# A narrow product as four column strips of TensorE, and a plan with its own durations for ACT and DVE, in a fused attention and MLP kernel

## The chip, the cores and the metric

One core of a Trainium2 chip. The metric is the device time of one execution in microseconds. The engines are named as the profile names them: PE (TensorE), PEld (its weight loads), DVE (VectorE), ACT (ScalarE), POOL (GpSimd), SP (SyncE). PSUM is the memory that takes the matmuls' results in this kernel; a ring is a fixed number of buffers that are used in turn. The granted clock is the share of PE's full clock that the profile records. The verdict "faster" begins at 2%.

## The reference

```python
# q, k, v: (8, 12, 448, 64) float32; U: (448, 32); V: (32, 448)
q_n = q / (norm(q) + 1e-6);  k_n = k / (norm(k) + 1e-6)
attn = softmax(q_n @ k_n.T / tau)
x = (attn @ v) with the heads side by side             # (8, 448, 768)
h = x.transpose(0, 2, 1) @ U @ V                       # low rank, over the sequence
u = x + h.transpose(0, 2, 1)
out = u + relu(u @ w_ch1) @ w_ch2                      # 768 -> 3072 -> 768
```

## The kernel before

The kernel does not issue instructions where it describes them. It adds operations to a plan; a list scheduler in Python gives each a start by estimated durations, and the instructions are issued in that order. The engines work through their own lists in order, so a number in the plan moves instructions on all of them. The plan counts buffers too: a matmul that takes a buffer of a ring waits in the plan until one is free. Cuts are marked with `# ...`.

```python
def pe_t(n):  return n / 2400.0 + 0.0025
def act_t(n, fixed=0.10):  return fixed + n * 0.00083
def dve_t(n, fast=1, fixed=0.16):  return fixed + n * 0.00104 / fast
# ...
r_mm = ring(3, [128, 512], FP, "mm", psum)      # three PSUM buffers: U, V, transposes, both MLP layers
r_sc = ring(3, [128, 512], FP, "sc", psum)      # three for the scores
U_sb = const.tile([128, 2, 4, 128], BF, name="U_sb")   # U's 32 columns, padded by zeros to 128
# ... in stage0(b), by column parts (512, 128, 128 in batches 0 and 1, 384, 384 later):
for t in range(4):                               # A = U^T x, summed over four parts of the sequence
    plan.add(Op("PE", pe_t(c1 - c0), lambda ...: nc.tensor.matmul(
        out=mm.tile[:, 0:c1 - c0], lhsT=U_sb[:, par, t, :], rhs=X.tile[:, t, c0:c1],
        start=(t == 0), stop=(t == 3)), ...))
a = Op("ACT/DVE", act_t(c1 - c0), None, ...)     # copy A out of PSUM; then V^T A, and u = x + it on DVE
# ... in mlp(b):
side = 3 if b == 0 else 1                        # output tiles of the second layer done together
# ... the constants:
nc.scalar.copy(out=U_sb[:, par, :, 0:R], in_=U_f()[:, par])
nc.scalar.copy(out=V_sb[0:R, PAD:PAD + S].rearrange("r (c s) -> r s c", c=SC),
               in_=V_f().rearrange("r (s c) -> r s c", c=SC))
```

Of the kernel before, what the change touches and what calls it, by code (L numbers as in the profile page):

```python
# [20 lines left out]
PAD = 64  # L21
# [28 lines left out]
class Plan:  # L50
# [5 lines left out]
    SEM = 0.10  # L56
    SAFE = 0.25

    def __init__(self):
# [40 lines left out]
    def run(self):  # L100
# [22 lines left out]
        while left:  # L123
# [6 lines left out]
            while progress:  # L130
                progress = False
                for e in self.ENGINES:
# [34 lines left out]
                    o.start, o.by = t, e  # L167
                    o.end = t + o.dur
                    free[e] = o.end
                    if isinstance(o.lat, tuple):  # L170
                        q, work, fixed = o.lat
                        dma[q] = max(dma[q], o.end) + work
                        o.end = dma[q] + fixed
                    else:
                        o.end += o.lat
# [23 lines left out]
def kernel(  # L199
# [79 lines left out]
    def U_f():  # L279
        return uv.tile[:, 0:8 * R].rearrange("p (b t r) -> p b t r", b=2, t=4)  # L280

    def V_f():
        return uv.tile[0:R, 8 * R:]

# [6 lines left out]

    U_sb = const.tile([128, 2, 4, 128], BF, name="U_sb")
    V_sb = const.tile([128, PAD + S + PAD], BF, name="V_sb")
# [25 lines left out]
    def pe_t(n):  # L319
        return n / 2400.0 + 0.0025  # L320

    def act_t(n, fixed=0.10):
        return fixed + n * 0.00083

    def dve_t(n, fast=1, fixed=0.16):
        return fixed + n * 0.00104 / fast

# [22 lines left out]
    def flip(stream, ins, n, into, part, deps, acq, rel):  # L350

        tp = Slot(r_mm, 1)
        tp.own = True
        for z, x in enumerate(ins):
            def fn(z=z, x=x):
                if z == 0:
                    tp.tile = psum.tile([128, len(ins), n], BF, name="tp", tag="mm", bufs=3)
                nc.tensor.transpose(out=tp.tile[:, z, :], in_=x(), identity=ident[:n, :n])  # L358
            o = plan.add(Op("PE", 0.06, fn, deps=deps + [id_set] if z == 0 else (), acq=[tp] + acq,
                            rel=rel if z == len(ins) - 1 else []), stream)  # L360
        c = plan.add(Op("ACT/DVE", dve_t(n * len(ins), 2), None, deps=[o], acq=acq, rel=[tp],
                        prio=0.2, fast=True))
        c.fn = lambda: copy_op(c, *part(into(), tp.tile))
        return c
# [36 lines left out]
    def load_v0(h0, h1):  # L401

        o = load(lambda: nc.gpsimd.dma_start(
            out=v_raw()[:, h0:h1, :], in_=v[0, h0:h1].rearrange("h (s c) d -> s h (c d)", c=SC)),
            (h1 - h0) * 0.5, acq=[raw])
        c = plan.add(Op("ACT/DVE", dve_t(256 * (h1 - h0), 2), None, deps=[o, v0_set], prio=0.35,
                        fast=True))
        c.fn = lambda: copy_op(c, v_first()[:, h0:h1, :, 0:D],
                               v_raw()[:, h0:h1, :].rearrange("p h (c d) -> p h c d", c=SC))
        for h in range(h0, h1):  # L410
            got[0, h, "v"] = [c]

    def stats(b, h0, h1, ld, ops):
# [5 lines left out]
        for i in range(2):  # L419
            for a0 in range(0, g, G // 2):  # L420
                a1 = min(g, a0 + G // 2)
                sq = Slot(r_sq, 1)
                o = Op("ACT/DVE" if b == 0 else "DVE", dve_t(256 * (a1 - a0), 2, 0.10), None,
                       deps=[ops[i]], acq=[sq], prio=pr + 0.2, fast=True)

                def square(o=o, i=i, a0=a0, a1=a1, sq=sq):
# [12 lines left out]
                    deps=[o], acq=[ss], rel=[sq], prio=pr + 0.1)))  # L439
        o = plan.add(Op("ACT", act_t(32), lambda: nc.scalar.activation(  # L440
            ln.tile[:, :, 0:g, :], ss.tile[:, :, 0:g, :], AF.Ln),
            deps=red, acq=[ln], rel=[ss], prio=0))
        o = plan.add(Op("ACT", act_t(32), lambda: nc.scalar.activation(
            nv.tile[:, :, 0:g, :], ln.tile[:, :, 0:g, :], AF.Exp, scale=0.5),
            deps=[o], acq=[nv], rel=[ln], prio=0))
        o = plan.add(Op("DVE", dve_t(32), lambda: nc.vector.tensor_scalar_add(
            nv.tile[:, :, 0:g, :], nv.tile[:, :, 0:g, :], EPS), deps=[o], prio=pr))
        o = plan.add(Op("DVE", dve_t(32), lambda: nc.vector.reciprocal(
            inv.tile[:, :, 0:g, :], nv.tile[:, :, 0:g, :]), deps=[o], acq=[inv], rel=[nv], prio=pr))
# [5 lines left out]
    def norm(b, p, ld, inv, a, deps, pr):  # L455
# [7 lines left out]
        def part(i, hh):  # L463
            def fn():
# [5 lines left out]
                else:  # L470
                    dst = xn.tile[:, 4 * hh:4 * hh + 4, 64 * hh:64 * hh + 64]
                    nc.vector.tensor_mul(dst, src[:, hh], sc[:, hh].to_broadcast([SCH, SC, D]))  # L472
            return plan.add(Op("DVE", dve_t(512 if i == 0 else 256, fixed=0.08), fn, deps=deps, acq=[xn],
                               rel=[ld, inv] if (i, hh) != (1, 0) else [ld, inv], prio=pr))
# [16 lines left out]
    def attention(b, p, X):  # L491
# [19 lines left out]
        for hh in range(2):  # L511
# [3 lines left out]
            for t in range(4):  # L515
                for j in range(4):
                    first, last = t == 0 and j == 0, t == 3 and j == 3
                    def fn(t=t, j=j, h=h, hh=hh, av=av):
# [8 lines left out]
                        rel=([attn, raw] if small and hh else [attn]) if last else []), pe_av)  # L527
            r = plan.add(Op("DVE", dve_t(4), lambda av=av, rd=rd: nc.vector.reciprocal(  # L528
                out=rd.tile, in_=av.tile[:, :, D:D + 1]), deps=[o], acq=[rd], prio=1))
# [4 lines left out]
        last_av[b, p] = o  # L534
        return muls


    prev = {}

    def stage0(b, X, muls):  # L540
# [5 lines left out]
        for c0, c1 in cols:  # L546
            mm = Slot(r_mm, 1)
            need = [m for i, m in enumerate(muls) if i * D < c1]
            for t in range(4):
                o = plan.add(Op("PE", pe_t(c1 - c0), lambda t=t, c0=c0, c1=c1, mm=mm: nc.tensor.matmul(  # L550
                    out=mm.tile[:, 0:c1 - c0], lhsT=U_sb[:, par, t, :], rhs=X.tile[:, t, c0:c1],
                    start=(t == 0), stop=(t == 3)),
                    deps=need + consts[:2 + par] if t == 0 else (), acq=[mm, A] if t == 0 else []),
                    pe_a if c1 < C else pe_av)
            a = Op("ACT/DVE", act_t(c1 - c0), None, deps=[o], rel=[mm], prio=0)
            a.fn = lambda a=a, c0=c0, c1=c1, mm=mm: copy_op(
# [64 lines left out]
    def mlp(b, us, uT, ut):  # L621
# [5 lines left out]
        for f in range(NC):  # L627
            mm = Slot(r_mm, 1)
            for cc in range(CC):
# [4 lines left out]
                    acq=[mm] if cc == 0 else [], rel=[uT]), pe_mlp)  # L634
            r = Op("ACT/DVE", act_t(n, 0.17), None, deps=[o], acq=[relu], rel=[mm],
                   prio=0)
# [64 lines left out]
    def zero():  # L701
        nc.vector.memset(U_sb, 0.0)
        nc.vector.memset(V_sb, 0.0)

    zf = fill(lambda: nc.vector.memset(U_f(), 0.0), 256, prio=-4, acq=[uv])
    z = fill(zero, 1500, prio=-0.2)

# [12 lines left out]
    def cast_u(par):  # L720
        nc.scalar.copy(out=U_sb[:, par, :, 0:R], in_=U_f()[:, par])

    def cast_v():
        nc.scalar.copy(out=V_sb[0:R, PAD:PAD + S].rearrange("r (c s) -> r s c", c=SC),
                              in_=V_f().rearrange("r (s c) -> r s c", c=SC))

# [17 lines left out]
    u0 = load_u(0)  # L744
    v0 = plan.add(Op("SP", 0.45, lambda: nc.sync.dma_start(out=V_f(), in_=moe_V), acq=[uv], prio=-2, lat=2.5))
    u1 = load_u(1)
# [8 lines left out]
    for i in range(NW):  # L755
        w1_ops.append(load_w1(i, NW))
    consts = [plan.add(Op("ACT", 0.25, lambda: cast_u(0), deps=u0 + [z], rel=[uv], prio=3)),
              plan.add(Op("ACT", 0.5, cast_v, deps=[v0, z], rel=[uv], prio=3)),
              plan.add(Op("ACT", 0.25, lambda: cast_u(1), deps=u1 + [z], rel=[uv], prio=3))]
# [55 lines left out]
```

## Time and profile before

| | before |
|---|---|
| median time | 628.89 us (628.43 to 629.86, 3 runs) |
| span of the profiled run | 625.9 us |
| PE, DVE, ACT busy | 95%, 50%, 46% |
| first matmul, first score matmul, first MLP matmul | 11.15, 13.58, 50.30 us |

The last row is read from PE's timeline. The chain's piece of MLP matmuls starts at 50.46. The batches go in pairs for the MLP; "the V stage" is the stretch in which batch 1's U, V and transposes run, near 92 to 104 us.

The windows of the kernel before, columns: window, length, busy us and count of PE, PEld, DVE, ACT and POOL, granted clock of PE, DMA share, GB/s.

```profile
85.00:95.00 10.00, 9.85 (x123) 6.45 (x121) 5.45 (x15) 7.91 (x18) 9.05 (x15) 1.00 1.40 113
95.00:105.00 10.00, 7.46 (x53) 4.48 (x52) 8.93 (x23) 2.78 (x5) 0.00 (x0) 0.83 0.10 7
105.00:115.00 10.00, 10.00 (x63) 6.00 (x62) 9.69 (x24) 0.92 (x4) 1.41 (x2) 1.00 0.59 83
```

In the second window PE is idle for a quarter of the time and its granted clock is 0.83 (0.50 from 99 to 101 us), while DVE is busy for nine tenths.

### The profile page before, as it was taken

How to read it: one execution, taken by the hardware profiler on the slowest of the kernel's cores; microseconds unless marked ns; L12 is line 12 of the kernel's file. 1: busy time of each engine (PE TensorE's matmuls, PEld its weight loads, DVE VectorE, ACT ScalarE, POOL GpSimd, SP SyncE). 2: the span in 40 equal slices, each digit the busy share in tenths (PEclk: the TensorE clock that was granted, in tenths of full speed). 3: DMA queues.
4: the chain of work that ended last, by engine and by line, in shares of the span. 5: the costliest groups of instructions: out<-in, count | busy, mean ns of one | idle time of the engine just before them, and what ended most of it. 6: DMA issues, size and time to landing. Idle time of an engine off the chain costs nothing.

```text
span 625.9 us, 11519 instructions
## 1 busy us (share of the span) xinstructions
PE 595.8 (95%) x4704; PEld 354.4 (57%) x4704; DVE 310.5 (50%) x763; ACT 286.2 (46%) x604; POOL 109.6 (18%) x168
## 2 busy tenths in 40 slices
PE   1799998999999999999999999999999999999997
PEld 1465665565555566666544666666544666654464
DVE  7876969999999888754650244014400220010011
ACT  6984782277874058424843048513543005104300
POOL 6227160152343303400320000000000000000000
PEclk9999998999999999999999999999999999999999
DMA  9999991999798968942781224030002310310011
GB/s 124 192 205 130 210 149 10 159 145 183 88 146 121 164 131 112 138 76 58 120 81 24 66 49 92 1 76 27 27 1 32 57 51 1 76 51 1 0 51 51
DMA packets 145733, 54.41 MB, mean 87 GB/s; under 512 B 109488, under 2 KB 145680, under 8 KB 145680
## 3 DMA queue, kind: packets, MB, share of 16 engines
q0 software_dynamic: 69216, 25.96, 37.2%
q1 hardware_dynamic: 76464, 27.71, 23.2%
q8 instruction: 37, 0.61, 0.4%
q14 instruction: 16, 0.13, 0.1%
HBM read 52.08 MB, written 11.01 MB: 101 GB/s over the span
## 4 chain that ended last, share of the span: by engine, by line
PE 81%; DVE 12%; ACT 3%; DMA 2%; SPq 1%; issue 1%; DVEq 0%; ACTq 0%
PE mm L630 32%; PE mm L653 30%; PE sc L503 9%; PE av L521 7%; DVE ss L435 2%; DVE xn L472 2%; PE mm L550 2%; DVE xn L469 1%; DVE sq L431 1%; PE mm L578 1%; ACT attn L507 1%; SPq L715 1%; DMA raw_uv<-in_moe_U_dram 1%; DMA out_dram<-O_sb 1%; DVE u_nat L592 1%; DVE X_sb L530 1%
## 5 line engine op out<-in xcount | busy, mean ns | idle before, releaser
L630 PE MATMUL mm<-uT,w_sb 128*128 128x512 bf16 (+1 forms) x1152 | 238.6, 353 | 1.2 <-DVE qkT L683 0.5
L653 PE MATMUL mm<-w_sb,relu 128*128 128x384 bf16 x1344 | 233.2, 326 | 1.5 <-DVE O_sb L663 0.7
L507 ACT ACTIVATE attn<-sc 128x448 bf16<-128x448 f32 (+1 forms) x342 | 160.8, 552 | 90.9 <-PE av L521 61.6
L653 PEld LDWEIGHTS <-relu 128*128 128x128 bf16 x1344 | 131.3, 98 | 92.6 <-issue 4.3
L630 PEld LDWEIGHTS <-w_sb 128*128 128x128 bf16 x1152 | 112.6, 98 | 104.5 <-issue 3.4
L640 ACT ACTIVATE relu<-mm 128x512 bf16<-128x512 f32 (+1 forms) x173 | 94.2, 545 | 158.6 <-PE mm L630 158.4
L663 DVE TENSOR_TENSOR O_sb<-mm,u_nat 128x384 f32<-128x384 f32 x56 | 30.8, 555 | 236.1 <-PE mm L653 231.7
L503 PE MATMUL sc<-qkT 128*128 128x448 bf16 (+1 forms) x342 | 102.3, 360 | 5.6 <-ACT attn L507 3.7
L521 PEld LDWEIGHTS <-attn 128*128 128x128 bf16 (+1 forms) x1536 | 61.0, 98 | 17.1 <-issue 2.9
L435 DVE TENSOR_REDUCE ss<-sq 112x8 f32<-112x512 bf16 x96 | 65.4, 683 | 4.3 <-ACT sq L429 1.7
L394 POOL DMA_DIRECT2D v_nat<-in_v_dram x98 | 63.1, 651 | 22.5 <-DMA w_sb<-in_moe_w_ch_dram 5.9
L521 PE MATMUL av<-v_nat,attn 128*128 128x65 bf16 x1344 | 55.1, 193 | 0.2
L372 POOL DMA_DIRECT2D qk_nat<-in_q_dram x25 | 17.8, 713 | 183.9 <-DVE rd L528 69.8
L503 PEld LDWEIGHTS <-qkT 128*128 128x128 bf16 (+1 forms) x342 | 32.1, 104 | 24.1 <-issue 5.7
L530 DVE TENSOR_TENSOR X_sb<-av,rd 128x256 bf16<-128x256 f32 x96 | 40.7, 424 | 3.3
L431 DVE TENSOR_TENSOR sq<-qk_nat 112x512 bf16<-112x512 bf16 x89 | 36.8, 413 | 0.0
L472 DVE TENSOR_TENSOR xn<-qk_nat,inv 112x256 bf16<-112x256 bf16 x96 | 36.3, 417 | 0.6
L469 DVE TENSOR_TENSOR xn<-qk_nat,inv 112x512 bf16<-112x512 bf16 x48 | 32.8, 682 | 0.0
L528 DVE RECIPROCAL rd<-av 128x4 f32<-128x4 f32 x96 | 17.0, 177 | 30.3 <-PE av L521 29.9
L592 DVE TENSOR_TENSOR u_nat<-mm,X_sb 128x384 bf16<-128x384 f32 (+2 forms) x54 | 25.1, 505 | 8.5 <-PE mm L578 8.4
L440 ACT ACTIVATE ln<-ss 112x32 f32<-112x32 f32 (+1 forms) x25 | 5.9, 234 | 39.5 <-DVE ss L435 38.3
L358 PE MATMUL tp<-ident,xn 112*128 112x112 bf16 x144 | 11.1, 231 | 11.9 <-DVE xn L472 11.2
(45 smaller groups left out, 184.7 us busy)
## 6 DMA issues: line engine op xcount, KB each, us to landing
qk_nat<-in_q_dram POOLq DMA_DIRECT2D x23, 224.0 KB, 5.5
qk_nat<-in_k_dram POOLq DMA_DIRECT2D x23, 224.0 KB, 6.7
w_sb<-in_moe_w_ch_dram POOLq DMA_DIRECT2D x4, 1152.0 KB, 19.2
w_sb<-in_moe_w_ch_dram POOLq DMA_DIRECT2D x8, 576.0 KB, 13.9
out_dram<-O_sb SPq DMA_DIRECT2D x16, 168.0 KB, 2.3
out_dram<-O_sb SPq DMA_DIRECT2D x16, 144.0 KB, 2.1
out_dram<-O_sb SPq DMA_DIRECT2D x16, 120.0 KB, 2.0
out_dram<-O_sb SPq DMA_DIRECT2D x16, 96.0 KB, 2.5
```

Of the source, the lines that this page charges most:

```text
L394: nc.gpsimd.dma_start(out=vb[p0:p0 + s1 - s0, hs, j, 0:D], in_=v[b, hs].rearrange("h (s c) d -> c s h d", c=SC)[c, s0:s1]),
L431: nc.vector.tensor_mul(y, x, x)
L435: lambda i=i, a0=a0, a1=a1, sq=sq: nc.vector.reduce_sum(ss.tile[:, i, a0:a1, :].rearrange("p h c -> p (h c)"), sq.tile[:, 0:a1 - a0, :].re ...
L469: nc.vector.tensor_mul(dst, src, sc.to_broadcast([SCH, 2, SC, D]))
L472: nc.vector.tensor_mul(dst, src[:, hh], sc[:, hh].to_broadcast([SCH, SC, D]))
L503: nc.tensor.matmul(out=sc.tile[0:rows_, 0:S], lhsT=kT[:, rows_ * m:rows_ * (m + 1)], rhs=qkT.tile[:, 8:12, :].rearrange("p c s -> p (c s)" ...
L507: exps[m] = plan.add(Op("ACT", act_t(S), lambda sc=sc, m=m: nc.scalar.activation(out=attn.tile[0:rows_, m, off:off + S], in_=sc.tile[0:row ...
L521: nc.tensor.matmul(out=av.tile[:, t, 0:D + 1], lhsT=attn.tile[0:rows_, m, 128 * t:128 * (t + 1)], rhs=vv[0:rows_, h, j, 0:D + 1], start=(j ...
L530: muls.append(plan.add(Op("DVE", dve_t(256), lambda av=av, rd=rd, h=h: nc.vector.tensor_mul(X.tile[:, :, h * D:(h + 1) * D], av.tile[:, :, ...
L630: o = plan.add(Op("PE", pe_t(n), lambda f=f, cc=cc, mm=mm: nc.tensor.matmul(out=mm.tile[:, 0:n], lhsT=w1_sb[:, cc, f * 128:(f + 1) * 128], ...
L640: nc.scalar.activation(out=relu.tile[:, f, 0:n], in_=mm.tile[:, 0:n], func=AF.Relu)
L653: nc.tensor.matmul(out=mm.tile[:, 0:CH], lhsT=relu.tile[:, f, i * 128:(i + 1) * 128], rhs=w2.tile[:, f, half * CH:(half + 1) * CH], start= ...
```

## The change

Its intent is twofold. U has 32 columns, a quarter of the 128 that the profile shows for the padded U (128*128), so the four parts of a sum can stand on four column strips and run at once; each leaves its 32 rows of the result, and V, repeated four times down the rows, adds them in its contraction. And the plan gets durations for ACT and DVE separately, and a lag between an operation's end and its result. The core of the diff (lines between those shown are left out):

```diff
+    LAG = {"PE": 0.16, "ACT": 0.10, "DVE": 0.07, "POOL": 0.0, "SP": 0.0}
-                    o.end = t + o.dur
+                    o.end = t + (o.dur[e] if isinstance(o.dur, dict) else o.dur)
                     free[e] = o.end
+                    o.end += self.LAG[e]
-    U_sb = const.tile([128, 2, 4, 128], BF, name="U_sb")
+    U_sb = const.tile([128, 2, 4, R], BF, name="U_sb")
-    def act_t(n, fixed=0.10):
+    def act_t(n, fixed=0.055):
-    def dve_t(n, fast=1, fixed=0.16):
-        return fixed + n * 0.00104 / fast
+    def dve_t(n, fast=1, fixed=0.065):
+        return fixed + n * 0.00105 / fast
+    def any_t(n, fast=1, fixed=0.065):
+        return {"ACT": act_t(n), "DVE": dve_t(n, fast, fixed)}
-                o = plan.add(Op("PE", pe_t(c1 - c0), lambda t=t, c0=c0, c1=c1, mm=mm: nc.tensor.matmul(
-                    out=mm.tile[:, 0:c1 - c0], lhsT=U_sb[:, par, t, :], rhs=X.tile[:, t, c0:c1],
-                    start=(t == 0), stop=(t == 3)),
+                o = plan.add(Op("PE", pe_t(c1 - c0) + 0.2 if t == 0 else 0.01,
+                                lambda t=t, c0=c0, c1=c1, mm=mm: nc.tensor.matmul(
+                    out=mm.tile[R * t:R * (t + 1), 0:c1 - c0], lhsT=U_sb[:, par, t, :],
+                    rhs=X.tile[:, t, c0:c1], start=True, stop=True),
-        nc.vector.memset(U_sb, 0.0)
         nc.vector.memset(V_sb, 0.0)
-    v0 = plan.add(Op("SP", 0.45, lambda: nc.sync.dma_start(out=V_f(), in_=moe_V), acq=[uv], prio=-2, lat=2.5))
+    v0 = [plan.add(Op("SP", 0.45, lambda t=t: nc.sync.dma_start(out=V_f()[R * t:R * (t + 1)], in_=moe_V),
+                      acq=[uv], prio=-2, lat=2.5)) for t in range(4)]
 # ... and the estimates of some twenty operations, among them any_t() for those that ACT or DVE may take
```

More of the change, by code (lines that the diff above doesn't have):

```diff
@@ L282, in V_f @@
     def V_f():
-        return uv.tile[0:R, 8 * R:]
+        return uv.tile[:, 8 * R:]
     r_O = ring(3, [128, CH], FP, "O_sb")
@@ L358, in fn @@
                 nc.tensor.transpose(out=tp.tile[:, z, :], in_=x(), identity=ident[:n, :n])
-            o = plan.add(Op("PE", 0.06, fn, deps=deps + [id_set] if z == 0 else (), acq=[tp] + acq,
+            o = plan.add(Op("PE", 0.05, fn, deps=deps + [id_set] if z == 0 else (), acq=[tp] + acq,
                             rel=rel if z == len(ins) - 1 else []), stream)
-        c = plan.add(Op("ACT/DVE", dve_t(n * len(ins), 2), None, deps=[o], acq=acq, rel=[tp],
+        c = plan.add(Op("ACT/DVE", any_t(n * len(ins), 2), None, deps=[o], acq=acq, rel=[tp],
                         prio=0.2, fast=True))
@@ L405, in load_v0 @@
             (h1 - h0) * 0.5, acq=[raw])
-        c = plan.add(Op("ACT/DVE", dve_t(256 * (h1 - h0), 2), None, deps=[o, v0_set], prio=0.35,
+        c = plan.add(Op("ACT/DVE", any_t(256 * (h1 - h0), 2), None, deps=[o, v0_set], prio=0.35,
                         fast=True))
@@ L422, in stats @@
                 sq = Slot(r_sq, 1)
-                o = Op("ACT/DVE" if b == 0 else "DVE", dve_t(256 * (a1 - a0), 2, 0.10), None,
+                o = Op("ACT/DVE" if b == 0 else "DVE", any_t(256 * (a1 - a0), 2, 0.17), None,
                        deps=[ops[i]], acq=[sq], prio=pr + 0.2, fast=True)
@@ L439, in stats @@
                     deps=[o], acq=[ss], rel=[sq], prio=pr + 0.1)))
-        o = plan.add(Op("ACT", act_t(32), lambda: nc.scalar.activation(
+        o = plan.add(Op("ACT", 0.25, lambda: nc.scalar.activation(
             ln.tile[:, :, 0:g, :], ss.tile[:, :, 0:g, :], AF.Ln),
             deps=red, acq=[ln], rel=[ss], prio=0))
-        o = plan.add(Op("ACT", act_t(32), lambda: nc.scalar.activation(
+        o = plan.add(Op("ACT", 0.2, lambda: nc.scalar.activation(
             nv.tile[:, :, 0:g, :], ln.tile[:, :, 0:g, :], AF.Exp, scale=0.5),
             deps=[o], acq=[nv], rel=[ln], prio=0))
-        o = plan.add(Op("DVE", dve_t(32), lambda: nc.vector.tensor_scalar_add(
+        o = plan.add(Op("DVE", 0.21, lambda: nc.vector.tensor_scalar_add(
             nv.tile[:, :, 0:g, :], nv.tile[:, :, 0:g, :], EPS), deps=[o], prio=pr))
-        o = plan.add(Op("DVE", dve_t(32), lambda: nc.vector.reciprocal(
+        o = plan.add(Op("DVE", 0.35, lambda: nc.vector.reciprocal(
             inv.tile[:, :, 0:g, :], nv.tile[:, :, 0:g, :]), deps=[o], acq=[inv], rel=[nv], prio=pr))
@@ L472, in fn @@
                     nc.vector.tensor_mul(dst, src[:, hh], sc[:, hh].to_broadcast([SCH, SC, D]))
-            return plan.add(Op("DVE", dve_t(512 if i == 0 else 256, fixed=0.08), fn, deps=deps, acq=[xn],
+            return plan.add(Op("DVE", dve_t(512 if i == 0 else 256), fn, deps=deps, acq=[xn],
                                rel=[ld, inv] if (i, hh) != (1, 0) else [ld, inv], prio=pr))
@@ L527, in attention @@
                         rel=([attn, raw] if small and hh else [attn]) if last else []), pe_av)
-            r = plan.add(Op("DVE", dve_t(4), lambda av=av, rd=rd: nc.vector.reciprocal(
+            r = plan.add(Op("DVE", 0.20, lambda av=av, rd=rd: nc.vector.reciprocal(
                 out=rd.tile, in_=av.tile[:, :, D:D + 1]), deps=[o], acq=[rd], prio=1))
@@ L549, in stage0 @@
             for t in range(4):
-                o = plan.add(Op("PE", pe_t(c1 - c0), lambda t=t, c0=c0, c1=c1, mm=mm: nc.tensor.matmul(
-                    out=mm.tile[:, 0:c1 - c0], lhsT=U_sb[:, par, t, :], rhs=X.tile[:, t, c0:c1],
-                    start=(t == 0), stop=(t == 3)),
+                o = plan.add(Op("PE", pe_t(c1 - c0) + 0.2 if t == 0 else 0.01,
+                                lambda t=t, c0=c0, c1=c1, mm=mm: nc.tensor.matmul(
+                    out=mm.tile[R * t:R * (t + 1), 0:c1 - c0], lhsT=U_sb[:, par, t, :],
+                    rhs=X.tile[:, t, c0:c1], start=True, stop=True),
                     deps=need + consts[:2 + par] if t == 0 else (), acq=[mm, A] if t == 0 else []),
                     pe_a if c1 < C else pe_av)
-            a = Op("ACT/DVE", act_t(c1 - c0), None, deps=[o], rel=[mm], prio=0)
+            a = Op("ACT/DVE", any_t(c1 - c0), None, deps=[o], rel=[mm], prio=0)
             a.fn = lambda a=a, c0=c0, c1=c1, mm=mm: copy_op(
@@ L634, in mlp @@
                     acq=[mm] if cc == 0 else [], rel=[uT]), pe_mlp)
-            r = Op("ACT/DVE", act_t(n, 0.17), None, deps=[o], acq=[relu], rel=[mm],
+            r = Op("ACT/DVE", any_t(n), None, deps=[o], acq=[relu], rel=[mm],
                    prio=0)
@@ L701, in zero @@
     def zero():
-        nc.vector.memset(U_sb, 0.0)
         nc.vector.memset(V_sb, 0.0)
     zf = fill(lambda: nc.vector.memset(U_f(), 0.0), 256, prio=-4, acq=[uv])
-    z = fill(zero, 1500, prio=-0.2)
+    z = fill(zero, 600, prio=-0.2)
     def load_u(par):
@@ L720, in cast_u @@
     def cast_u(par):
-        nc.scalar.copy(out=U_sb[:, par, :, 0:R], in_=U_f()[:, par])
+        nc.scalar.copy(out=U_sb[:, par], in_=U_f()[:, par])
     def cast_v():
-        nc.scalar.copy(out=V_sb[0:R, PAD:PAD + S].rearrange("r (c s) -> r s c", c=SC),
-                              in_=V_f().rearrange("r (s c) -> r s c", c=SC))
+        nc.scalar.copy(out=V_sb[:, PAD:PAD + S].rearrange("r (c s) -> r s c", c=SC),
+                       in_=V_f().rearrange("r (s c) -> r s c", c=SC))
     w1_ops, w2_ops = [], []
@@ L757 @@
     consts = [plan.add(Op("ACT", 0.25, lambda: cast_u(0), deps=u0 + [z], rel=[uv], prio=3)),
-              plan.add(Op("ACT", 0.5, cast_v, deps=[v0, z], rel=[uv], prio=3)),
+              plan.add(Op("ACT", 0.5, cast_v, deps=v0 + [z], rel=[uv], prio=3)),
               plan.add(Op("ACT", 0.25, lambda: cast_u(1), deps=u1 + [z], rel=[uv], prio=3))]
```

## The prediction

> **What bounds the kernel now.** I read the split of busy time first, then the chain that ended last, then windows cut where the work changes, then the timelines. From the page, engine shares and the chain:
>
> ```profile
> PE 595.8 (95%) x4704; PEld 354.4 (57%) x4704; DVE 310.5 (50%) x763; ACT 286.2 (46%) x604; POOL 109.6 (18%) x168
> ...
> PE 81%; DVE 12%; ACT 3%; DMA 2%; SPq 1%; issue 1%; DVEq 0%; ACTq 0%
> ```
>
> TensorE (PE) is busy 95% of the span and owns 81% of the chain. But matmuls are pipelined, so I asked what one matmul occupies. From the timeline of PE:
>
> ```profile
> 137.48 0.81 PE L550 MATMUL mm<-X_sb,U_sb 128*128 128x384 bf16 x4
> 138.13 0.67 PE L521 MATMUL av<-v_nat,attn 128*128 128x65 bf16 x16
> 138.65 0.54 PE L503 MATMUL sc<-qkT 128*128 128x448 bf16 x2
> ```
>
> The four U matmuls of one group begin at 137.48 and the next group at 138.13: 0.65 us, so 0.1625 us a matmul, though one lasts 0.326 us from start to end (its row of the groups). The other 0.164 us is pipeline that the next matmul covers. Likewise 16 attention-times-V matmuls take 0.52 us, 0.032 each. From such rows the slots are: 512 columns 0.216, 448 columns 0.189, 384 columns 0.1625, 128 columns 0.056, 112 columns 0.049, 65 columns 0.032 us. Times the counts by shape: 592 x 0.216 + 342 x 0.189 + 2016 x 0.1625 + 74 x 0.056 + 144 x 0.049 + 1536 x 0.032 = 580 us. The span is 626, so 46 us are not streaming. Where? The windows, cut at the first matmul, the first MLP matmul of the first pair of batches (50.46) and the first score matmul after its second layer began (120.18):
>
> ```profile
> 0.00:11.15 11.15, 0.00 (x0) 0.00 (x0) 7.67 (x27) 6.49 (x10) 6.34 (x14) 1.00 0.88 109
> 11.15:50.46 39.31, 31.86 (x352) 21.81 (x353) 30.83 (x81) 32.19 (x68) 13.64 (x20) 0.96 1.26 190
> 50.46:120.18 69.72, 64.94 (x594) 40.99 (x592) 58.51 (x144) 36.80 (x82) 25.06 (x37) 0.98 0.98 131
> 120.18:620.00 499.82, 497.24 (x3752) 290.74 (x3750) 212.97 (x513) 210.69 (x446) 64.58 (x98) 1.00 0.50 73
> ```
>
> With the same slots, the matmuls that stand ahead of the one at 50.46 need 22 us, those from there to 120.18 need 60, the rest 498. So the losses are about 28 us (11 before the first matmul, 17 in batch 0, where ACT is busy 32.2 and DVE 30.8 of 39.3 us), 10 us up to 120, and 7.5 us in the 506 us after that, of which 4.2 are the last output's way out. **From 120 us on the kernel is bound by PE streaming alone; before it, by ACT, DVE and waits.** A change can win by removing PE slots, or by shortening the first 120 us.
>
> [...] after the stall at 94 to 99 us five 384-column matmuls take 0.320 us instead of 0.1625.
>
> **The change, part by part.**
>
> 1. *Column strips.* 72 U matmuls in 18 groups of four (12 of 384 columns, 2 of 512, 4 of 128), nothing added: V has the same 72 matmuls, and its contraction of 128 rows costs what the padded one did. Before, a group takes 4 slots: 0.65, 0.86, 0.22 us. After, I estimate one slot[...]: 0.39 to 0.50 for 384, 0.45 to 0.55 for 512, 0.29 to 0.39 for 128 columns. Savings: 0.15 to 0.26, 0.31 to 0.41, and minus 0.07 to minus 0.17 us. The order of the changed kernel's instructions shows two groups split 1 + 3 by an attention group in between (one of 512, one of 384)[...]. Sum: 11 x 0.2 + 0.35 - 4 x 0.12 - 0.5 = **about 1.6 us saved** (0.8 to 2.5). The upper limit, with free switches, is three quarters of 12 x 0.65 + 2 x 0.86 + 4 x 0.22 = 10.4, that is 7.8 us.
>
> 2. *Constants.* U's tile no longer needs its 0.48 us memset on DVE. V now arrives in four copies by four transfers: three more on the queue of SP, where an issue takes 0.4 to 0.6 us. This matters, because ACT's queue is in order and it waited for U's last transfer. From the chain of the first 17 us:
>
> ```profile
> 7.85 0.81 SPq L715
> 8.71 5.98 DMA raw_uv<-in_moe_U_dram
> 14.78 0.30 ACT U_sb L721
> 15.08 0.53 ACT sq L429
> 15.61 0.44 ACT attn L507
> ```
>
> U's last piece was issued at 8.71 and landed at 14.69; ACT stood 1.06 us at its cast, and the first exponentials came behind it. Three more issues put this at most 1.6 us later: estimated loss 0.5 to 1 us.
>
> 3. *The plan.* Nearly all of ACT's and DVE's order shifts, but the engines' work stays. What I can read from the order: (a) V's cast (2.18 us on ACT, at 6.28, ahead of the second square) now stands behind all four early squares and the first logarithm and exponential, so the first norms come sooner: estimated 0.5 us. (b) Up to the first MLP matmul ACT loses the 1.9 us copy of the raw v (to DVE) and three copies of 896 columns, and gets 4 more squares of about 0.55 and some copies of 448: about -1 us of 42; DVE about even. As ACT's and DVE's work is the limit there, and both idle a fifth of the time, I put 1 to 2 us on finer interleaving. (c) Later, first-layer work goes ahead of the transposes (80 matmuls instead of 74), and the second layer of the first pair starts before batch 1's V stage, filling PE while DVE finishes. The V stage itself lost 4.8 us (80 to 100 us), as its adds are 5.4 us of DVE work; here 1 to 2 us. (d) After 120 us at most 3 us are there to win; I count 0.5.
>
> Sum: 1.6 - 0.7 + 0.5 + 1.5 + 1.5 + 0.5 = 4.9 us off 628.9, so **624 us**.
>
> **Rivals.** *R1, the strips run one after the other, or each pays a switch.* For it: nothing in this trace shows concurrency, and the order alternates modes 18 times or more. Against:[...] that the four matmuls stand together in 16 groups. Then a group costs 0.65 + 0.33 and PE grows by some 6 us: 632 to 635. *R2, the plan is what counts and saves far more than the strips.* For it: 38 us are lost before 120 us. Against: 11 of them are loads and norms of the first heads that no order shortens much, and ACT and DVE are each busy four fifths of 11 to 50 us. A good plan could win 8 us: 617. *R3, the tighter plan is off in the wrong places.* It has less slack for transfers that land late (5.98 us where the plan takes 2.5), so in-order queues wait more; the early gain turns to a loss of 2 to 4 us: 630. *R4, the saved PE time is hidden anyway.* Speaks against: from 120 us on PE is 99% busy, so each slot saved there shows in full.
>
> **Range and chances.** The strips' term is -2.5 to +1 for most cases, the plan's -8 to +4. Together 8 in 10: 616 to 631. Faster by over 2% needs under 616.3, which takes R2 in full with the strips at their best: 0.11. Slower by over 2% (over 641) takes R1 and R3 together: 0.02. Within 2%: 0.87.
>
> **What would show it.** The U group of 384 columns in PE's timeline: next start after 0.39 to 0.50 us (step 1 right), about 0.25 (switches free) or above 0.65 (R1). The cast of U waiting beyond 15 us (step 2). First matmul before 11 us (3a). First MLP matmul at 48 to 50 us instead of 50.46 (3b), less half-clock and idle PE at the V stage (3c); 120 to 620 as full as now (3d). I am wrong if the first 120 us move by over 5 us in either direction, or if the switch costs much more than one pipeline depth.

The forecast's sum came to 4.9 us and so to 624 us with terms that are cut here. They stand in step 1, in its 1.6 us: in each group's estimate up to 0.164 us on each side, for the way into and out of the strips, and some issue time; and the 0.5 us for the two split groups, which pay these ways twice. The 0.164 us was the estimate from the trace before (one matmul of 384 columns lasts 0.326 us, its slot is 0.1625). That four strips take about one slot was an assumption as well; the next section has it measured.

## More of the kernel before

One measure is used from here on, **lost time**: the start of a matmul, less the slots (start to next start when nothing waits) of all matmuls ahead of it in the order. It is counted from the instruction order and not from the records, because 24 matmul records are missing from the changed kernel's trace and none from the one before. Before, it is 28 us at the first MLP matmul, 30.5 at 90 us, 37.9 at 120 us and 41.3 at the end of PE's work. So the V stage and what follows up to 120 us lose 7.4 us.

## The result, and the profile after

The changed kernel takes **621.63 us** in the median (620.91 to 622.36, 4 runs), against 628.66 before in the same rounds. The ratio is 0.9889, with a 95% interval of 0.9865 to 0.9912. A ratio here is the mean time of one kernel's fast runs over that of the other's of the same rounds, so it is not quite the ratio of the medians. The verdict is "same": 1.1% faster, under the 2% line.

The U group in the changed kernel's timeline of PE, between two other groups:

```profile
154.40 0.35 PE L508 MATMUL sc<-qkT 128*128 128x448 bf16 x1
154.59 0.59 PE L638 MATMUL mm<-uT,w_sb 128*128 128x512 bf16 x2
155.11 0.35 PE L558 MATMUL mm<-X_sb,U_sb 128*32 128x384 bf16 x4
155.39 0.55 PE L508 MATMUL sc<-qkT 128*128 128x448 bf16 x2
```

Four matmuls of 384 columns now last 0.35 us together, barely more than one (0.33), and the next group starts 0.28 us after the first, where it was 0.65. Singly, the four start 3 to 4 ns apart. What I call the switch shows ahead of them: the two MLP matmuls of 512 columns began at 154.59 and would be through their slots at 155.02; the strips start at 155.11, 0.09 us later. The padded U of the kernel before has no such gap (its first U matmul at 137.48 starts one slot, 0.162 us, after the matmul ahead of it). In the 0.28 us there is another 0.1 beyond one slot, which I count as the way out. So a group costs 0.37 us (0.28 + 0.09; the expectations below say 0.38) instead of 0.65 and saves 0.28, a factor of about 1.75.

The windows of the changed kernel over the V stage:

```profile
85.00:95.00 10.00, 10.00 (x113) 6.59 (x113) 5.05 (x14) 4.93 (x11) 5.78 (x9) 1.00 1.24 89
95.00:105.00 10.00, 8.48 (x58) 4.87 (x56) 6.36 (x15) 0.99 (x4) 0.00 (x0) 1.00 0.12 37
105.00:115.00 10.00, 7.49 (x39) 4.17 (x40) 9.57 (x26) 2.18 (x3) 1.42 (x2) 0.52 0.36 77
```

The stage has moved 10 us later, and it is worse: in the third window PE is idle for a quarter of the time and runs at half clock for nearly all of it (granted 0.52 on average, and 0.50 from 106 to 115 us, after 3 us from 103 on in which PE was busy for 1.11). Its longest idle time in that stage is 1.57 us; what sets the clock no run here separates. Its timeline says what it waits for:

```profile
92.59 9.75 PE L661 MATMUL mm<-w_sb,relu 128*128 128x384 bf16 x59
102.67 0.24 PE L558 MATMUL mm<-X_sb,U_sb 128*32 128x128 bf16 x4 [0.32 <-DVE O_sb L671]
103.27 0.24 PE L558 MATMUL mm<-X_sb,U_sb 128*32 128x128 bf16 x4 [0.36 <-ACT A_sb L689]
103.44 0.77 PE L586 MATMUL mm<-A_sb,V_sb 128*128 128x512 bf16 x4
105.78 0.29 PE L586 MATMUL mm<-A_sb,V_sb 128*128 128x128 bf16 x1 [1.57 <-DVE u_nat L597]
```

The second layer of the first pair (L661) works on three output tiles at once and holds all three buffers of the mm ring until DVE has added its output (O_sb, L671). The U and V matmuls need the same ring, and each V matmul then waits for a buffer that DVE empties (u_nat, L597).

### The profile page after: what moved, and what is told of

Its sections match the earlier page's. It is cut to its first block, busy times and chain, and to the rows that moved or that the text cites. A ratio compares the mean times of both kernels' runs of the same rounds, so it can differ in the third digit from the quotient of the medians.

```text
span 619.8 us, 11510 instructions
## 1 busy us (share of the span) xinstructions
PE 590.7 (95%) x4680; PEld 348.5 (56%) x4704; DVE 297.1 (48%) x754; ACT 286.8 (46%) x612; POOL 109.7 (18%) x168
## 4 chain that ended last, share of the span: by engine, by line
PE 86%; ACT 4%; DVE 4%; DMA 2%; SPq 1%; issue 1%; DVEq 0%; ACTq 0%
PE mm L638 34%; PE mm L661 33%; PE sc L508 9%; PE av L526 7%; ACT attn L512 3%; DMA out_dram<-O_sb 1%; PE tp L363 1%; DVE u_nat L600 1%; PE mm L586 1%; DMA raw_uv<-in_moe_V_dram 1%; PE mm L558 1%; DVE O_sb L671 1%; DVE xn L477 1%; SPq L722 1%; DVE xn L474 0%
## 5 line engine op out<-in xcount | busy, mean ns | idle before, releaser
L638 PE MATMUL mm<-uT,w_sb 128*128 128x384 bf16 (+1 forms) x1130 | 234.4, 352 | 1.0
L661 PE MATMUL mm<-w_sb,relu 128*128 128x384 bf16 x1344 | 234.9, 327 | 0.4 <-ACT uT L689 0.4
L512 ACT ACTIVATE attn<-sc 128x448 bf16<-128x448 f32 (+1 forms) x342 | 165.1, 558 | 84.5 <-PE av L526 55.6
L661 PEld LDWEIGHTS <-relu 128*128 128x128 bf16 x1344 | 131.6, 98 | 89.1 <-issue 1.8
L648 ACT ACTIVATE relu<-mm 128x512 bf16<-128x512 f32 (+1 forms) x175 | 95.5, 546 | 151.3 <-PE mm L638 151.0
L671 DVE TENSOR_TENSOR O_sb<-mm,u_nat 128x384 f32<-128x384 f32 x56 | 30.8, 555 | 233.8 <-PE mm L661 226.5
L508 PE MATMUL sc<-qkT 128*128 128x448 bf16 (+1 forms) x342 | 103.9, 357 | 7.1 <-DVE qkT L691 3.5
L440 DVE TENSOR_REDUCE ss<-sq 112x8 f32<-112x512 bf16 x96 | 63.0, 672 | 0.5 <-ACT sq L434 0.2
L436 DVE TENSOR_TENSOR sq<-qk_nat 112x512 bf16<-112x512 bf16 x85 | 32.4, 410 | 0.0
L586 PE MATMUL mm<-A_sb,V_sb 128*128 128x384 bf16 (+2 forms) x70 | 18.5, 322 | 3.8 <-DVE u_nat L597 2.1
```

The costliest lines, as they stand in the source:

```text
L440: lambda i=i, a0=a0, a1=a1, sq=sq: nc.vector.reduce_sum(ss.tile[:, i, a0:a1, :].rearrange("p h c -> p (h c)"), sq.tile[:, 0:a1 - a0, :].re ...
L508: nc.tensor.matmul(out=sc.tile[0:rows_, 0:S], lhsT=kT[:, rows_ * m:rows_ * (m + 1)], rhs=qkT.tile[:, 8:12, :].rearrange("p c s -> p (c s)" ...
L512: exps[m] = plan.add(Op("ACT", act_t(S), lambda sc=sc, m=m: nc.scalar.activation(out=attn.tile[0:rows_, m, off:off + S], in_=sc.tile[0:row ...
L638: o = plan.add(Op("PE", pe_t(n), lambda f=f, cc=cc, mm=mm: nc.tensor.matmul(out=mm.tile[:, 0:n], lhsT=w1_sb[:, cc, f * 128:(f + 1) * 128], ...
L648: nc.scalar.activation(out=relu.tile[:, f, 0:n], in_=mm.tile[:, 0:n], func=AF.Relu)
L661: nc.tensor.matmul(out=mm.tile[:, 0:CH], lhsT=relu.tile[:, f, i * 128:(i + 1) * 128], rhs=w2.tile[:, f, half * CH:(half + 1) * CH], start= ...
```

## The experiments

Every kernel here gave correct results. All ran five rounds beside the kernel before on the same chip, in four sets: strips_old_order, full_new_order, "changed, again" and late_casts; gathered, side1, v_first and v_cast; serial_strip, sc_ring and late_vcast; best. The kernel before took 628.24, 628.09, 628.34 and 627.66 us in them. Ratios compare across sets, medians only within one. "First score" and "first MLP" are times in PE's timeline; "lost, 90 to 120" is the growth of the lost time from 90 to 120 us.

| run | median us | ratio to before (95%) | first score | first MLP | lost, 90 to 120 |
|---|---|---|---|---|---|
| before | 628.24 (11 runs, first set) | 1 | 13.58 | 50.30 | 7.4 |
| changed, again | 621.49 | 0.9891 (0.9873 to 0.9909) | 15.36 | 47.49 | 9.3 |
| strips_old_order | 625.20 | 0.9954 (0.9939 to 0.9970) | 14.21 | 50.25 | 8.4 |
| full_new_order | 623.45 | 0.9925 (0.9910 to 0.9939) | 14.42 | 47.63 | 8.4 |
| serial_strip | 629.68 | 1.0026 (1.0009 to 1.0043) | 14.26 | 50.45 | 7.7 |
| gathered | 620.12 | 0.9878 (0.9861 to 0.9894) | 16.08 | 47.96 | 8.9 |
| late_casts | 620.86 | 0.9887 (0.9868 to 0.9905) | 12.99 | 47.87 | 8.5 |
| v_cast | 621.31 | 0.9897 (0.9878 to 0.9915) | 14.74 | 48.73 | 9.9 |
| late_vcast | 619.82 | 0.9869 (0.9850 to 0.9888) | 13.24 | 46.94 | 8.5 |
| side1 | 620.10 | 0.9872 (0.9856 to 0.9888) | 16.02 | 48.05 | 7.5 |
| v_first | 620.72 | 0.9883 (0.9862 to 0.9904) | 16.03 | 48.00 | 7.6 |
| sc_ring | 617.73 | 0.9835 (0.9819 to 0.9851) | 16.02 | 51.64 | 1.6 |
| best | **610.36** | **0.9720 (0.9697 to 0.9743)** | 13.45 | 46.06 | 1.0 |

(The profile row of "changed, again" is that of the first run of the changed kernel; the repeat's own profile has 15.35, 47.32 and 9.0. The kernels gathered and side1 have its early ACT work in the same order, and their first MLP matmul came at 47.96 and 48.05: half a microsecond there, and 0.3 us of lost time, is noise of one profile.)

### Which half carries the gain

**strips_old_order.** The strips and the new constants, with the order of the kernel before on every engine. To hold the order, the plan keeps its old numbers, and V's four transfers are one operation in it.

```diff
 # in the kernel before:
-                    out=mm.tile[:, 0:c1 - c0], lhsT=U_sb[:, par, t, :], ... start=(t == 0), stop=(t == 3)),
+                    out=mm.tile[R * t:R * (t + 1), 0:c1 - c0], lhsT=U_sb[:, par, t, :], ... start=True, stop=True),
+    def load_v_const():
+        for t in range(4):
+            nc.sync.dma_start(out=V_f()[R * t:R * (t + 1)], in_=moe_V)
```

> The column strips and the constants in their new form, with every engine's order exactly as in the kernel before (checked: the orders differ only in the shapes of the U matmuls and of the casts, and in U's memset). Theory A (PE slots alone): 11 unsplit 384 groups after 120 us shrink by the 0.27 us that the changed kernel's trace shows (0.65 to 0.38, its switch included), the split one by nothing, the early ones lie beside waits: 2.5 to 3.5 us less, ratio 0.995. Rival B (the strips carry nearly all of the gain): ratio 0.989. Rival C (three more V transfers eat the strips' gain): ratio 0.998 to 1.002, with ACT standing longer at the casts of U and V.

Measured: 0.9954, 2.9 us off. That is theory A.

**full_new_order.** The opposite half: the changed kernel's order, with U padded to 128 columns again and V loaded once.

```diff
 # in the changed kernel, the plan's numbers kept:
-                    out=mm.tile[R * t:R * (t + 1), 0:c1 - c0], ... start=True, stop=True),
+                    out=mm.tile[:, 0:c1 - c0], ... start=(t == 0), stop=(t == 3)),
```

> The order of the changed kernel on every engine, with U 128 columns wide again (padded by zeros, four matmuls accumulating), V once. Theory A: the plan alone is worth what the strips do not explain, 3.5 to 4 us, so ratio 0.994 to before, and about 3 us over the changed kernel. Rival B (strips carry all): ratio 0.998 to 1.002. Rival R2 (plan carries all): ratio 0.989.

Measured: 0.9925, 4.7 us off: the plan is the larger half, and neither rival holds.

**after_again.**

> The changed kernel in the same rounds, as the yardstick: ratio 0.989 again. If the parts add up, (1 minus ratio of strips alone) plus (1 minus ratio of plan alone) is 0.011; a sum clearly below it means that the parts need each other (the plan counts with short U groups), a sum above it that they overlap.

Measured: 0.9891. The parts give 0.0046 + 0.0075 = 0.0121 against 0.0109 together, which the intervals do not tell apart. The parts add, or overlap a little.

### Is it the concurrency?

**serial_strip.** U is 32 columns wide, but all four matmuls go to the first strip and accumulate there; V uses 32 rows. Order as before.

```diff
-                    out=mm.tile[R * t:R * (t + 1), 0:c1 - c0], ... start=True, stop=True),
+                    out=mm.tile[0:R, 0:c1 - c0], ... start=(t == 0), stop=(t == 3)),
```

> The order of the kernel before, and U's four matmuls of a group 32 output columns wide as in the change, but all on the first column strip, accumulating there one after the other (V uses rows 0 to 31 alone, the rest of it and of A is zero). It keeps the switch of the array's tiling and takes the concurrency away. Theory (the gain is that four strips stream at once): a 384 group takes 0.65 us from first start to next start plus about 0.09 of entry, against 0.28 plus 0.09 with four strips; the kernel is 1 to 2 us slower than before (18 groups by 0.1), ratio 1.001 to 1.004, and 4 to 5 us slower than the same order with four strips. Rival (narrow matmuls are cheap by themselves): a group takes well under 0.65 us and the ratio is below 1.

Measured: 1.0026, and 4.5 us over the same order with four strips (625.20, another set). PE's timeline, the same place in the order, serial and then with four strips:

```profile
137.88 0.49 PE L654 MATMUL mm<-w_sb,relu 128*128 128x384 bf16 x2
138.29 0.82 PE L551 MATMUL mm<-X_sb,U_sb 128*32 128x384 bf16 x4
139.05 0.62 PE L522 MATMUL av<-v_nat,attn 128*128 128x65 bf16 x14
```

```profile
137.49 0.49 PE L653 MATMUL mm<-w_sb,relu 128*128 128x384 bf16 x2
137.90 0.35 PE L550 MATMUL mm<-X_sb,U_sb 128*32 128x384 bf16 x4
138.18 0.72 PE L521 MATMUL av<-v_nat,attn 128*128 128x65 bf16 x16
```

From first start to the next group it is 0.76 us against 0.28. The entry is the same in both: 137.88 to 138.29 is 0.41 us, two slots of 0.1625 and 0.09. With it a serial group costs 0.85 us, 0.2 more than before, where 0.1 was expected. So narrow matmuls alone gain nothing and pay the switch (0.09 us ahead of the group, and 0.76 - 4 x 0.1625 = 0.11 behind it); all of the saving is the four at once.

**gathered.** The changed kernel in its order, but the two U groups that the plan splits 1 + 3 around an attention group are issued whole. The plan keeps its four operations; the first three issue nothing.

> The changed kernel in exactly its order, but the two U groups that the plan splits 1 + 3 around an attention group (one of 512, one of 384 columns) are issued whole, where the second part stood. Theory: each split costs a second way into and out of the strips, read from the changed kernel's trace as 0.745 us against 0.383 for the whole 384 group and 0.86 against 0.47 for the 512 group. So 0.4 to 0.8 us less than the changed kernel, ratio to before 0.988. Rival: no difference, because the plan's slack takes it up; then the time of the changed kernel within 0.2 us.

Measured: 620.12 against 621.49 for the changed kernel, in other rounds. The difference of 1.4 us is more than expected, but the intervals of the two ratios overlap, so the times alone show no gain. The trace supports the direction: the whole 384 group reads 0.28 us from first start to next start, as the others do, where the two parts of the split one read 0.27 and 0.28 us, with an entry of 0.09 each.

### The first 50 us

In the changed kernel the first scores come later than before (15.36 against 13.58 us) although the first transposes come sooner. ACT's timeline in the changed kernel:

```profile
9.30 0.30 ACT L728 CAST U_sb<-raw_uv 128x128 bf16<-128x128 f32 x1
10.88 2.19 ACT L731 CAST V_sb<-raw_uv 128x448 bf16<-128x448 f32 x1 [1.28 <-DMA raw_uv<-in_moe_V_dram]
12.57 0.51 ACT L445 ACTIVATE ln<-ss 112x16 f32<-112x16 f32 x1
12.64 1.30 ACT L689 COPY raw_v<-raw_v 112x1024 bf16<-112x1024 bf16 x1
13.83 0.22 ACT L448 ACTIVATE ln<-ln 112x16 f32<-112x16 f32 x1
15.01 0.30 ACT L728 CAST U_sb<-raw_uv 128x128 bf16<-128x128 f32 x1 [0.96 <-DMA raw_uv<-in_moe_U_dram]
```

V's fourth transfer, issued behind seven of U's, keeps ACT waiting for 1.28 us, the cast takes 2.19, and the logarithm and the exponential that the second heads need stand behind it. DVE waits 2.79 us for that exponential, with the copies of the first transposes behind it in its queue.

**late_casts.**

```diff
-                    deps=[zf], prio=-2, lat=2.5)))     # U's transfers
+                    deps=[zf], prio=-2, lat=12.0)))    # and the same for V's
```

> The changed kernel, but the plan counts 12 us instead of 2.5 for the transfers of U and V, so that ACT's casts of them stand later in its queue. In the changed kernel the first scores start at 15.36 us, because ACT waits 1.28 us for V's fourth transfer, casts for 2.2 us, and the first logarithms, then DVE's copies, stand behind that. Theory: the first scores start at 12.5 to 13.5 us and the first MLP matmul comes 1 to 2 us earlier than 47.5: ratio 0.985 to 0.988. The plan also moves batch 1's V stage ahead of the second layer, which could give 2 us more. Rival (ACT and DVE are the limit up to 47 us and a wait at 10 us is made up later): first MLP matmul within 0.5 us of 47.5.

Measured: the first scores at 12.99 us, 2.4 us sooner, and the first MLP matmul at 47.87, not sooner at all. The rival holds. The lost time shows where the lead goes: 15.4 against 17.0 us at 20 us, 17.7 against 18.7 at 25 us, and 21.0 against 20.6 at 30 us. The cast, which had stood in a stretch of waits, now stands at 22 us among the exponentials:

```profile
20.71 1.43 ACT L512 ACTIVATE attn<-sc 112x448 bf16<-112x448 f32 x3
21.98 2.24 ACT L731 CAST V_sb<-raw_uv 128x448 bf16<-128x448 f32 x1
23.68 0.91 ACT L512 ACTIVATE attn<-sc 112x448 bf16<-112x448 f32 x1
```

**v_cast.** Only the loops of V's cast are swapped.

```diff
-        nc.scalar.copy(out=V_sb[:, PAD:PAD + S].rearrange("r (c s) -> r s c", c=SC),
-                       in_=V_f().rearrange("r (s c) -> r s c", c=SC))
+        nc.scalar.copy(out=V_sb[:, PAD:PAD + S].rearrange("r (c s) -> r c s", c=SC),
+                       in_=V_f().rearrange("r (s c) -> r c s", c=SC))
```

> The changed kernel in exactly its order; only the loops of V's cast on ACT are swapped, so that its inner run is 112 elements long instead of 4. Here it takes 2.19 us, while ACT casts 512 columns of A in 0.58. Theory: about 0.5 us for the cast; ACT is the limit up to 47 us, so the first MLP matmul comes 1 to 1.7 us earlier than 47.5, ratio 0.986 to 0.9875. Rival (DVE or the waits are the limit there): first MLP matmul within 0.4 us of 47.5. If the cast stays near 2.2 us, strides are not what it pays for.

Measured: the cast fell from 2.19 to 0.98 us, not to the 0.5 expected (the swap also makes the writes contiguous instead of the reads, and no run separates the two), and nothing was gained; the first MLP matmul even came at 48.73 us, 1.2 later and outside both ranges given. ACT's timeline:

```profile
11.28 0.98 ACT L731 CAST V_sb<-raw_uv 128x448 bf16<-128x448 f32 x1 [0.90 <-DMA raw_uv<-in_moe_V_dram]
12.17 0.21 ACT L445 ACTIVATE ln<-ss 112x16 f32<-112x16 f32 x1
12.28 1.03 ACT L689 COPY raw_v<-raw_v 112x1024 bf16<-112x1024 bf16 x1
13.22 0.21 ACT L448 ACTIVATE ln<-ln 112x16 f32<-112x16 f32 x1
15.56 0.30 ACT L728 CAST U_sb<-raw_uv 128x128 bf16<-128x128 f32 x1 [2.13 <-DMA raw_uv<-in_moe_U_dram]
```

A wait took its place: the next cast waited 2.13 us for U instead of 0.96. In this profile U also landed some 0.55 us later (the cast starts at 15.56 instead of 15.01), which no edit explains, so the later first MLP matmul is not shown to come from the swap.

**late_vcast.** Both together.

> The changed kernel with both: the casts of U and V counted later (as late_casts) and V's cast in the fast loop order (0.98 us instead of 2.19). Each alone gave under 0.7 us: the late cast moved 2.2 us of ACT work into the stretch where ACT is the limit, the fast cast left ACT waiting longer for U's transfer. Theory (ACT is the limit up to the first MLP matmul, waits included): together the first scores start near 13.0 us and the first MLP matmul at 46.0 to 46.8 us instead of 47.5 to 47.9; ratio 0.985 to 0.9865. Rival (something else bounds the first stage): within 0.3 us of late_casts, ratio 0.9885.

Measured: first scores at 13.24 and the first MLP matmul at 46.94, 0.14 us above the expected range; the ratio of 0.9869 is 0.0004 above its range too. The direction is the theory's, and the time is 1.0 us under late_casts (another set), though within the intervals. Best, below, has the same casts and its first MLP matmul at 46.06, against 47.96 and 48.05 in gathered and side1. That ACT's work limits this stretch is supported by these profiles, and not shown by the times.

### The V stage

**side1.** `side = 1` for all batches, so that the block of 72 no longer takes the whole ring.

> The changed kernel, with the second layer of the first pair done one output tile at a time (one PSUM buffer of the mm ring) instead of three at once. In the changed kernel that block of 72 matmuls holds all three buffers from 91 to 102 us and batch 1's U and V stage comes behind it, with 9 us of PE lost between 102 and 115. Theory (the block pushes the V stage to where nothing runs beside it): the V stage moves ahead and interleaves, 2 to 4 us less than the changed kernel, ratio 0.983 to 0.986. Rival (the V stage is bound by DVE's 5.4 us of adds and three buffers wherever it stands): the same loss of 6 to 9 us at another place, ratio 0.988 to 0.990.

Measured: the V stage moved ahead, to 95 us, and lost 7.5 us there instead of 9.3. Ratio 0.9872, between the theory's range and the rival's 0.988 to 0.990. PE's timeline:

```profile
95.92 0.93 PE L586 MATMUL mm<-A_sb,V_sb 128*128 128x512 bf16 x4
97.40 0.22 PE L586 MATMUL mm<-A_sb,V_sb 128*128 128x128 bf16 x1 [0.55 <-DVE u_nat L600]
98.00 0.22 PE L586 MATMUL mm<-A_sb,V_sb 128*128 128x128 bf16 x1 [0.38 <-DVE u_nat L600]
```

The V matmuls still wait for DVE one by one, with nothing between them. The place is not the cause of the 7.5 us; the other 1.8, about what the change had added, did go with it, in one profile.

**v_first.** The V matmuls of the first 512 columns ahead of the second U group in batches 0 and 1.

> The changed kernel, with the V matmuls of the first 512 columns put ahead of the U group of columns 512 to 640 in PE's stream for batches 0 and 1, so that DVE's adds of those columns can run while attention still goes on. Theory: batch 1's loss between 90 and 120 us falls from 9.3 to 5 to 7 us, ratio 0.983 to 0.986. Rival as for the run before: unchanged, 0.988 to 0.990.

Measured: 7.6 us lost, 0.9883: the rival again.

**sc_ring.** As side1, and the U and V matmuls of batches 0 and 1 write to the scores' three PSUM buffers.

```diff
-            mm = Slot(r_mm, 1)
+            mm = Slot(r_sc if by_pe else r_mm, 1)      # for the U groups, and the same for the V groups
```

> The changed kernel with the second layer of the first pair one tile at a time (as side1), and with the U and V matmuls of batches 0 and 1 writing to the three PSUM buffers of the scores instead of the three that MLP uses. Theory (the 7 to 9 us lost around batch 1's V stage are there because it and the MLP want the same three buffers, so nothing runs beside DVE's adds): MLP matmuls interleave with V, the loss between 88 and 125 us falls from 8 to 9 us to 2 to 4, the kernel takes 614 to 616 us, ratio 0.978 to 0.982. Rival (DVE or ACT is the limit there, whatever the buffers): 619 to 621 us.

Measured: 1.6 us lost instead of 9.3, and instead of 7.5 in side1, from which its edit differs by the ring alone (the plan's order was made anew); that is below the expected 2 to 4. PE's timeline shows what fills it:

```profile
94.37 0.38 PE L586 MATMUL sc<-A_sb,V_sb 128*128 128x512 bf16 x1
94.58 0.49 PE L638 MATMUL mm<-uT,w_sb 128*128 128x384 bf16 x2
94.91 0.28 PE L586 MATMUL sc<-A_sb,V_sb 128*128 128x128 bf16 x2
95.02 0.65 PE L638 MATMUL mm<-uT,w_sb 128*128 128x384 bf16 x3
95.51 0.22 PE L586 MATMUL sc<-A_sb,V_sb 128*128 128x128 bf16 x1
95.56 0.65 PE L638 MATMUL mm<-uT,w_sb 128*128 128x384 bf16 x3
```

The same V matmuls, with MLP matmuls of the other ring between them. DVE's adds are unchanged, so the rival (DVE or ACT is the limit whatever the buffers) falls. The time, 617.73 us, missed the expected 614 to 616, because batch 0 had the scores' buffers too: its scores then waited for its own V stage, and the first MLP matmul came at 51.64 us instead of 47.49.

**best.** Everything that helped, with the scores' ring for batch 1 alone: gathered, side1, late_vcast, and

```diff
+            mm = Slot(r_sc if b == 1 else r_mm, 1)
```

> All that helped, together: the changed kernel with whole U groups, the second layer of the first pair one tile at a time, the scores' PSUM buffers for the U and V matmuls of batch 1 alone (in sc_ring batch 0 had them too, and its scores then waited: first MLP matmul at 51.64 us instead of 47.49), and the casts of U and V later and in the fast loop order. If the gains lie at separate places they add: first MLP matmul near 47 us (as late_vcast), 1.5 to 3 us lost around batch 1's V stage (as sc_ring), 612 to 614 us, ratio 0.974 to 0.978. Rival (the early stages are one chain through ACT and DVE, so what one part saves another waits for): 616 to 618 us, as sc_ring.

Measured: **610.36 us, 0.9720**, beyond the expected range of 612 to 614: 17 us under before in the same rounds (627.66) and 11 under the changed kernel. The windows of this kernel over the V stage:

```profile
85.00:95.00 10.00, 9.94 (x103) 6.53 (x103) 7.63 (x19) 3.94 (x9) 5.46 (x9) 1.00 1.17 80
95.00:105.00 10.00, 9.67 (x79) 5.89 (x79) 9.95 (x28) 2.56 (x7) 0.00 (x0) 1.00 0.14 41
105.00:115.00 10.00, 10.00 (x64) 6.02 (x62) 9.05 (x20) 0.47 (x3) 1.41 (x2) 1.00 1.18 169
```

PE is nearly full and at full clock (granted 1.00), with DVE nearly full beside it.

## Why the prediction was right or wrong, point by point

The total was right: 624 predicted with a range of 616 to 631, 621.6 measured, "within 2%" the favoured class. The steps did less well than the sum.

- *Step 1, the strips.* Right in mechanism, too small in size. The term was 1.6 us (0.8 to 2.5); strips and constants alone measured 2.9 us, with step 2's loss already in it. The mis-sized term is the switch: my estimate took all of what a matmul lasts beyond its slot, 0.164 us, on each side, and it measured 0.09 on the way in and about 0.1 on the way out; what it consists of no run shows. A 384 group costs 0.37, just under my 0.39 to 0.50, and saves 0.28. The other term that I had too large is the splitting, 0.5 for two groups: with both entries the split 384 group costs 0.73 us against 0.65 before, so it loses 0.1, and the split 512 group still costs no more than before. A weight load took 0.093 us with 32 columns, 0.098 with 128; whether one lies in the 0.09 us of entry no run shows. V's matmuls of 384 columns cost the same as before (0.325 us from start to end, 0.326 before). My test in terms of the next start was put badly: 0.28 us is what follows the first start, and the entry stands ahead of it.
- *Step 2, the constants.* The waits for U and V that I feared are there (1.28 and 0.96 us). But the loss of 0.5 to 1 us is not shown: taking the wait away (late_casts) or shortening the cast (v_cast) moved no more than the noise, and in strips_old_order, with the new constants in the old order, the first scores came 0.6 us later (14.21) but the first MLP matmul no later (50.25). The stretch has other waits, and what is lost at 15 us is made up by 50.
- *Step 3a, V's cast.* Half right. The first matmul came at 10.41 instead of 11.15 us. What I missed is that the cast then stands ahead of the second heads' logarithm and waits for a transfer: the first scores were 1.8 us later.
- *Step 3b, interleaving up to the first MLP matmul.* Right, undersized: 47.49 against 50.30, where I gave 48 to 50. In full_new_order it is 47.63, so this is the plan, not the strips.
- *Step 3c, the V stage.* This step failed. I counted 1 to 2 us of gain from "the second layer of the first pair starts before batch 1's V stage, filling PE while DVE finishes". The runs showed the opposite: the lost time from 90 to 120 us grew from 7.4 to 9.3 us. The filler holds all three PSUM buffers that the V stage needs, so nothing of that stage can overlap with it, and PE idles afterwards, at half clock (2.5 of the 10 us from 105 on, granted 0.52). The shared buffers are the cause of most of the loss: 7.5 us stay when the block is taken one tile at a time (side1) and 7.6 when V goes earlier (v_first), 1.6 when the V stage gets other buffers (sc_ring). Of the growth from 7.4 to 9.3, side1 took 1.8 us back in one profile, so that part may be the block's.
- *Step 3d, after 120 us.* Undersized: with the plan alone the lost time grows by 1.9 us from 120 us to the end, before by 3.4, so 1.5 us instead of 0.5.
- *Rivals.* R1 (serial strips) is refuted by the trace and sized by serial_strip. R2 (the plan saves 8 us) was too strong, but its direction was better than my weights: the plan is 4.7 of 7 us. R3 (a tighter plan waits longer for late transfers) happened at 10 to 15 us (the waits for V and U of 1.28 and 0.96 us) and was made up by 47. R4 (hidden anyway) is refuted by strips_old_order.

So the total owed something to errors that cancelled: steps 1, 3b and 3d were too small, 3c had the wrong sign. From sc_ring to best it is 7.4 us (medians of different sets, as are those that follow): batch 0's later start (51.64 - 47.49 = 4.2), late_vcast (1.7 under the changed kernel) and gathered (1.4) come to 7.2 or 7.3 of it, though the plan was rebuilt for each, and no run separates a better order from the removed waits. What stays open is why the V stage loses 8.4 us with either half of the change alone, but 9.3 with both (9.0 in the repeat) and 7.4 with neither.

## What to carry to other kernels

In these runs the array's strips pay only when they stream at once (a 384 group costs 0.37 us with four at once, 0.85 one after the other and 0.65 at full width), and each visit costs a switch of some 0.2 us (0.09 in, about 0.1 out), so keep the strips' matmuls together and do not alternate. Where a scheduler plans the order, it isn't enough that it counts the buffers, as this one does: work that "fills" an idle engine fills nothing if it takes the ring that the waiting stage needs; ask which ring is idle at that moment. And a wait removed ahead of a loaded engine can come back further on, as late_casts shows; see whether that engine's own work can be cut as well.
